# Filling TensorE in the head of a fused delta-rule and GELU kernel: early loads, products that nobody reads, a later weight transfer

## The chip, the cores and the metric

The kernel runs on one core of a Trainium2 chip. The metric is the device time of one execution, in microseconds (us). The kernel before takes 625.35 us, the median of 3 runs from 625.1 to 626.43 us. The engines are named as in the profile: PE (matrix products; PEld is its weight load), DVE (vector), ACT (scalar), POOL (GpSimd) and SP, which issues most transfers.

## The reference

```python
# q, k, v: (4, 8, 768, 48); beta: (4, 8, 768)
k_n = k / (np.linalg.norm(k, axis=-1, keepdims=True) + 1e-06)
state = np.zeros((B, H, D, D), dtype=np.float32)
for t in range(S):
    kt, vt, bt = (k_n[:, :, t], v[:, :, t], beta[:, :, t, None])
    y[:, :, t] = np.einsum('bhd,bhde->bhe', q[:, :, t], state)
    v_old = np.einsum('bhde,bhd->bhe', state, kt)
    state = state + bt[:, :, :, None] * np.einsum('bhd,bhe->bhde', kt, vt - v_old)
...
x = y.transpose(0, 2, 1, 3).reshape(B * S, H * D)      # (3072, 384)
h = x @ w_in                                           # w_in (384, 2048), float64 on input
g = 0.5 * h * (1.0 + erf(h * inv_sqrt2))
out = (g @ w_out).astype(np.float32)                   # w_out (2048, 384), float64 on input
```

The attention is a delta rule over 768 steps for 32 heads; its outputs are the tokens of a two-layer network with an exact GELU.

## The kernel before

**Chunks and units.** The 768 steps are cut into 12 chunks `c` of 64. A unit (`tiles[c, a]`) is one chunk of two batches: batch p of the pair sits on half p of the 128 partitions. Two chunks make a group `g`. `first` are the four units of chunks 0 and 1, `third` the two of chunk 2, `fourth` the two of chunk 3.

**Inside a group.** K is transposed on PE (`transposed`, L405) and multiplied with itself (`diagonals` for the 32x32 diagonal blocks of group 0, `grams` for the rest) and with Q (`queries`). Each 64x64 triangular system is inverted in two halves of 32: `eliminate_steps` (L491) scales a triangle (`scales`, on POOL), turns the diagonal blocks (`flip`, DVE L508, L513), goes through rows j = 1 to 30 with two small DVE instructions each (L528, L530), and turns the result back (`back`, L536): `back(0)` into XM, `back(1)` into the right columns of `Zf`, and in group 0 `back(2)` into the left columns of `Zf`, all three DVE transposes of 128x1024. `clear` then sets the lower left quarter of `Zf` to zero. `join` (L568) couples the two halves: at level 0 PE products that DVE scales into XM (L589), at level 1 PE products that ACT copies into `Zf` (L593). `against_state`, `solve` (psU), `use` (psY), `update` (psS) and `turn` (psX) then give the chunk's outputs, turned for the network.

**The network.** `fc1` (L909) makes psH from `w_in_sb` and the turned outputs, followed by a GELU on ACT into `G`; `fc2` (L929) makes psO from `G` and `w_out_sb`. From chunk 2 on the layers are done with fewer products, out of sums of blocks (`part_of_layer`, `second_layer`).

**The weights.** They arrive as float64 and are decoded to float32 by integer steps. A part `n` (0 to 7 of w_in, from `n_in` = 8 of w_out) goes through `fetch` (its transfers, L234), `begin` (exponent bits, DVE L252 or L255), `exponents` (ACT), `mantissas` (two DVE steps, L272 and L274) and `signed` (L281 and L282, after which the buffer is fetched into again). Where `two_kinks(n)` holds, ACT does the exponent in two steps and `signed` has no L281. The raws of w_in 0 to 3 wait in `w_out_sb`, those of w_out in `w_raw` slots.

**Order.** Up to `by_hand.close()` the order on DVE, POOL, ACT, PE and SP is that of the program text. After it a list of steps with due times (`plan`, in units of chunks) is sorted and emitted; DVE and POOL keep that order, and so does ACT where `keep` is used, while PE, SP and the rest of ACT are ordered by a scheduler, except for runs tied by `together` and `behind`. In the head SP issues, in this order: K of chunks 0, 1, beta, Q of chunks 0, 1, V of chunk 0, raws 0, 1 of w_in, K of chunk 2, Q of chunk 2 (into the buffers of chunk 0's Q), K of chunk 3 (into `Qp[2 + a]`), raws 2, 3 of w_in, raws 0 to 2 of w_out, V of chunk 1.

Of the kernel before, what the change touches and what calls it, by code (L numbers as in the profile page):

```python
# [19 lines left out]
def kernel(  # L20
# [165 lines left out]
    G = Gp[0]  # L186
    spare = Gp[1].rearrange("q a f n -> q (a f n)")
# [51 lines left out]
    def two_kinks(n):  # L239

        return 2 < n < n_in or n_in + 3 < n < n_in + 7
# [27 lines left out]
    def mantissas(n):  # L269
        dst, lo, hi, e = halves[n]  # L270
        bits = dst.bitcast(U32)
        nc.vector.tensor_scalar(bits, hi, 0xFFFFF, 0x100000, op0=ALU.bitwise_and,  # L272
                                op1=ALU.bitwise_or)
        nc.vector.scalar_tensor_tensor(dst, lo, 2.0 ** -32, bits, ALU.mult, ALU.add)  # L274
# [24 lines left out]
    def decode_in():  # L299

        marks = {3: (None, 1.05, 0.99, 1.06), 4: (1.0, 1.09, 1.1, 1.13),
                 5: (1.12, 1.18, 1.14, 1.2), 6: (1.19, 1.24, 1.21, 1.25),
                 7: (1.245, 1.3, 1.29, 1.36)}
        steps = []
        for n, (a, b, c, d) in marks.items():
            if a is not None:
                steps += [(a, (begin, n))]
            steps += [(b, (exponents, n, keep)), (c, (mantissas, n)), (d, (signed, n))]
        return steps
# [95 lines left out]
    def transposed(u, part=(0, 1)):  # L405
        for x in part:
# [10 lines left out]
            flat = (Qp[2 + u.a] if u.c == 3 and x == 0 else (u.Kp, u.Qp)[x]).rearrange("q h d -> q (h d)")  # L417
# [73 lines left out]
    def eliminate_steps(g):  # L491
# [44 lines left out]
        def back(x):  # L536
# [4 lines left out]
            elif x == 1 or g == 0:  # L541
                cols = slice(HB, C) if x == 1 else slice(0, HB)
                nc.vector.transpose(Zf[g % 2][:, :, cols].rearrange("q u i -> q i u"), nu)
# [8 lines left out]
        def clear(g):  # L552
                for cc in range(2):
                    for p in range(2):
                        part = Zf[g % 2][p * C + HB:(p + 1) * C,
                                         cc * NU // 2:(cc + 1) * NU // 2, 0:HB]
                        if g == cc == p == 0:
                            nc.scalar.mul(part, low[0:HB, 0:HB // 2], 0.0)
                        else:
                            nc.gpsimd.memset(part, 0.0)  # L560

# [3 lines left out]
        steps += [(1.9, back, x) for x in range(3)]  # L565
        return steps + [(0.0, clear, 0)] if g == 0 else steps
# [342 lines left out]
    def fc1(c, f):  # L909
# [8 lines left out]
        if c <= 1 or f < EARLY:  # L918
            keep(nc.scalar.activation, *gelu)
        else:  # L920
            nc.scalar.activation(*gelu)
# [270 lines left out]
    def signs(c0, c1):  # L1192
# [7 lines left out]

    by_hand = ExitStack()
    by_hand.enter_context(tc.manual_schedule(engines={
        mybir.EngineType.DVE, mybir.EngineType.Pool, mybir.EngineType.Activation,
        mybir.EngineType.PE, mybir.EngineType.SP}))
    load_v(0)
    for n in range(2):
        fetch(n)
    load_k(2, "Kp")
    new_group(0)
    n0 = wk.tile([128, 2 * NA, H], F32, tag="n0", name="n0", bufs=1)  # L1210
    for c in range(2):
        ns[c] = n0[:, c * NA:(c + 1) * NA]
    for u in first:
        squares(u, n0[:, u.t], nc.gpsimd if u.t == 1 else nc.vector)
        transposed(u, (0,))
        if u.t in (1, 2):
            diagonals(first[u.t - 2 + 1])
# [4 lines left out]
    scales_, flip_, *rows, back0, back1, back2, clear_ = [s_[1:] for s_ in eliminate_steps(0)]  # L1222
    factors(gms[0], beta_m[:, 0:2].rearrange("q c a h -> q (c a) h"), n0)
    scales_[0]()
    flip_[0]()
# [3 lines left out]
    signs(2, NC)  # L1229
    third = [tiles[2, a] for a in range(NA)]  # L1230
    sums_ = [(u, h) for u in third for h in range(H)]
    for u in first:
        transposed(u, (1,))
        if u.c == 1:
            for x in sums_[5 * u.a:5 * u.a + 5]:
                sum_of_squares(*x)
        queries([u])
    for a in range(NA):
        fetch_q(tiles[2, a])
    for a in range(NA):  # L1240
        fetch_in(Qp[2 + a][:, :, 0:D], k, tiles[3, a])
    for n in range(2, NS):
        fetch(n)
    for n in range(n_in, n_in + 3):
        fetch(n)
    load_v(1)
    for u in third:
        transposed(u, (0,))
    for x in sums_[10:13]:
        sum_of_squares(*x)  # L1250
    grams(third)
    for u in third:
        transposed(u, (1,))
    for x in sums_[13:]:
        sum_of_squares(*x)
    fourth = [tiles[3, a] for a in range(NA)]
    for u in fourth:
        transposed(u, (0,))
    grams(fourth)
    for fn, *args in rows:  # L1260
        fn(*args)
    nc.vector.scalar_tensor_tensor(ng, gms[0][:, 0:NA], -1.0, ns[0], ALU.mult, ALU.mult)
    back0[0](*back0[1:])
    against_state(first[:NA])
    for u in first:
        masked(u)
    back1[0](*back1[1:])
    for a in range(NA):
        join(0, (a,), 0)
    back2[0](*back2[1:])  # L1270
    for a in range(NA):
        join(0, (a,), 1)
    clear_[0](*clear_[1:])
    for u in first[NA:]:
        scale_v(u)
    begin(0)
    exponents(0)
    mantissas(0)
# [30 lines left out]
    def state_at(c, *times, first=(), second=(), last=()):  # L1309

        steps = state_steps(c, first, second, last)
        if len(times) > len(steps):
# [7 lines left out]
    plan += [at(1.06, 1.065, [(1.0, load, 3)]),  # L1320
             [(t, (join, 0, range(NA, 2 * NA), level)) for level, t in enumerate((1.085, 1.16))],
# [20 lines left out]
    plan += [at(1.36, 1.361, [(1.0, fetch, n_in + 3)]), at(1.07, 1.071, [(1.0, load_v, 2)]), at(2.727, 2.728, [(1.0, sum_of_w, 1, 2)]), at(2.96, 2.961, [(1.0, last_sum_of_w)]), at(3.07, 3.071, [(1.0, sum_of_w, 4)])]  # L1342
# [129 lines left out]
```

## Time and profile before

| | |
|---|---|
| median of 3 runs | 625.35 us (625.1 to 626.43) |
| profiled execution | 626.68 us, span 624.9 us |
| PE busy | 602.5 us (96%), mean granted clock 0.989 |
| DVE busy | 440.1 us (70%) |
| ACT busy | 241.4 us (39%) |
| POOL busy | 212.6 us (34%) |
| chain that ended last | PE 81%, DVE 14%, issue 2%, DMA 1%, ACT 1% |
| from HBM, to HBM | 33.62 MB, 4.72 MB |

Busy time is a share of the whole span; the head, up to some 75 us, has other limits than the rest, so it is read by the timelines of each engine and by windows. In a timeline a row is a run of like instructions: start, time taken, engine, line, operation, tiles, shapes, count, and in brackets the idle time of the engine before it and what ended it. "issue" there means that the profile shows nothing that the engine waited for. An fp32 product counts twice (two passes) in the trace, a transpose on PE once.

### The profile page before, as it was taken

The page shows a single profiled execution, that of the slowest core. Times are in us where ns is not written, and L with a number is a line of the kernel's source. Part 1 is how long each engine was busy: PE and PEld are TensorE (multiplying, and loading weights), DVE is VectorE, ACT ScalarE, POOL GpSimd, SP SyncE. Part 2 cuts the span into 40 slices and gives each one's busy share as a digit, 9 for nine tenths or more (in the row PEclk, how much of TensorE's full clock was granted, in tenths as well). Part 3 has the DMA queues.
Part 4 walks back from the last instruction along what each step waited for, and adds up shares of the span by engine and source line. Part 5 has one row for each costly group of instructions (what it writes and reads, how often), then busy time and mean ns, then how long its engine had stood idle before and what let it go on. Part 6 is the DMA issues. An engine that isn't in the chain of part 4 may idle for free.

```text
span 624.9 us, 19704 instructions
## 1 busy us (share of the span) xinstructions
PE 602.5 (96%) x8358; PEld 537.7 (86%) x8358; DVE 440.1 (70%) x811; ACT 241.4 (39%) x546; POOL 212.6 (34%) x316
## 2 busy tenths in 40 slices
PE   5768999999999999999999999999999999999997
PEld 4657786776899998998899998899998899988997
DVE  6999899999967697774859755859745947332532
ACT  3576877625443264224451134451134222044200
POOL 4045002100379821687222885222885200000000
PEclk9996999999999999999999999999999999999999
DMA  9793775002423452353123533013421001010011
GB/s 134 164 294 118 174 179 149 17 10 40 72 38 49 77 93 37 57 115 39 16 43 55 95 70 39 13 29 52 79 50 17 12 3 27 3 24 1 0 27 26
DMA packets 159576, 39.64 MB, mean 63 GB/s; under 512 B 151168, under 2 KB 154368, under 8 KB 159488
## 3 DMA queue, kind: packets, MB, share of 16 engines
q1 hardware_dynamic: 156816, 37.34, 30.9%
q10 hardware_dynamic: 2672, 1.03, 0.9%
q8 instruction: 66, 1.08, 0.7%
q14 instruction: 22, 0.18, 0.1%
HBM read 33.62 MB, written 4.72 MB: 61 GB/s over the span
## 4 chain that ended last, share of the span: by engine, by line
PE 81%; DVE 14%; issue 2%; DMA 1%; ACT 1%; SPq 0%; DVEq 0%
PE psX L966 13%; PE psY L1032 11%; PE psY L966 9%; PE psX L1032 9%; PE psV L1032 6%; PE psZ L1032 6%; PE psZ L966 4%; PE psV L966 4%; DVE tmp L528 3%; DVE Nu L530 3%; PE psK L732 3%; PE psO L933 3%; PE psH L915 2%; PE psY L822 2%; PE psU L792 2%
## 5 line engine op out<-in xcount | busy, mean ns | idle before, releaser
L377 POOL TENSOR_TENSOR n<-n,half 128x16 f32<-128x16 f32 x10 | 31.4, 3138 | 180.1 <-DVE n L375 130.0
L530 POOL TENSOR_TENSOR Nu<-Nu,tmp 128x30 f32<-128x30 f32 (+14 forms) x120 | 65.0, 541 | 9.4
L528 POOL TENSOR_TENSOR tmp<-Nu 128x30 f32<-128x30 f32 (+14 forms) x120 | 62.4, 520 | 9.4
L1032 PE MATMUL psX<-xT,w_in_sb 128*128 128x256 f32 (+1 forms) x288 | 62.6, 346 | 0.0
L966 PE MATMUL psX<-w_out_sb,G 128*128 128x192 f32 x320 | 56.1, 329 | 0.0
L966 PEld LDWEIGHTS psX<-w_out_sb,G 128*128 128x128 f32 x320 | 52.2, 190 | 0.7
L1032 PEld LDWEIGHTS psX<-xT,w_in_sb 128*128 128x128 f32 x288 | 47.9, 190 | 5.4
L915 PE MATMUL psH<-xT,w_in_sb 128*128 128x256 f32 x192 | 44.7, 387 | 0.7 <-ACT G L1015 0.5
L933 PE MATMUL psO<-w_out_sb,G 128*128 128x384 f32 x128 | 43.9, 490 | 0.0
L851 DVE TENSOR_TENSOR V<-psY,y 64x192 f32<-64x192 f32 (+1 forms) x60 | 21.3, 355 | 31.0 <-PE psY L834 27.0
L915 PEld LDWEIGHTS psH<-xT,w_in_sb 128*128 128x128 f32 x192 | 36.2, 192 | 7.9 <-ACT G L1015 2.3
L1060 DVE TENSOR_TENSOR psY<-psY,pu 128x512 f32<-128x512 f32 x20 | 14.0, 700 | 40.5 <-PE psY L1032 39.9
L1032 PE MATMUL psY<-xT,w_in_sb 128*128 128x256 f32 (+1 forms) x192 | 41.5, 345 | 0.0
L1015 ACT COPY xT<-psX 128x768 f32<-128x768 f32 x9 | 7.2, 799 | 79.8 <-PE psX L892 79.8
L1015 ACT COPY pu<-psZ 128x512 f32<-128x512 f32 x40 | 23.5, 587 | 37.3 <-PE psZ L1032 35.0
L933 PEld LDWEIGHTS psO<-w_out_sb,G 128*128 128x128 f32 x128 | 23.6, 190 | 14.1
L1032 PEld LDWEIGHTS psY<-xT,w_in_sb 128*128 128x128 f32 x192 | 32.1, 191 | 3.5
L1015 ACT ACTIVATE G<-G 128x512 f32<-128x512 f32 x40 | 25.2, 631 | 21.0 <-DVE G L1068 20.8
L1068 DVE TENSOR_TENSOR G<-psY,pu 128x512 f32<-128x512 f32 x20 | 13.8, 691 | 22.2 <-PE psY L1032 21.5
L1015 ACT ACTIVATE G<-psY 128x512 f32<-128x512 f32 x20 | 11.9, 596 | 45.3 <-PE psY L1032 45.3
L966 PE MATMUL psY<-w_out_sb,G 128*128 128x192 f32 x160 | 28.1, 329 | 0.0
L966 PE MATMUL psZ<-T,pu 128*128 128x192 f32 x160 | 28.1, 329 | 0.0
(207 smaller groups left out, 1370.2 us busy)
## 6 DMA issues: line engine op xcount, KB each, us to landing
Kp<-in_k_dram SPq DMA_DIRECT2D x76, 96.0 KB, 3.2
w_out_sb<-in_moe_w_in_dram SPq DMA_DIRECT2D x24, 256.0 KB, 4.0
V<-in_v_dram SPq DMA_DIRECT2D x48, 96.0 KB, 3.1
w_raw<-in_moe_w_out_dram SPq DMA_DIRECT2D x12, 384.0 KB, 7.4
out_dram<-o_sb SPq DMA_DIRECT2D x40, 96.0 KB, 2.2
Qp<-in_k_dram SPq DMA_DIRECT2D x64, 32.0 KB, 2.3
G<-in_moe_w_out_dram SPq DMA_DIRECT2D x4, 384.0 KB, 5.1
Qp<-in_q_dram SPq DMA_DIRECT2D x96, 16.0 KB, 2.0
```

The costliest lines, as they stand in the source:

```text
L377: nc.gpsimd.tensor_tensor(flat, flat, half, op=ALU.pow)
L528: rows_on.tensor_tensor(tmp, nu[:, j + 1:, j:j + 1].to_broadcast([128, n, j]), nu[:, j:j + 1, 0:j].to_broadcast([128, n, j]), op=ALU.mult)
L530: rows_on.tensor_tensor(nu[:, j + 1:, 0:j], nu[:, j + 1:, 0:j], tmp, op=ALU.add)
L732: nc.tensor.matmul(u.psK[HALF[p], r, j, :], lhsT=u.Kt[rows, p, j, :], rhs=SQ[rows, u.a, p ^ r, j, 0:w], start=True, stop=True)
L851: nc.vector.tensor_tensor(dst, src, pairs(u.y[at_], s), op=ALU.add)
L915: nc.tensor.matmul(psH, lhsT=w_in_sb[:, f // 2, m, f % 2 * 128:(f % 2 + 1) * 128], rhs=xTs[c][:, m, :], start=(m == 0), stop=(m == NM - 1))
L933: nc.tensor.matmul(u.psO, lhsT=G[:, u.a, f, :], rhs=w_out_sb[:, f, :], start=(f == 0), stop=(f == NF - 1))
L966: nc.tensor.matmul(ps_, lhsT=lhs[:, f, :], rhs=rhs[:, f, :], start=first and f == 0, stop=f == FH - 1, skip_group_check=not first)
L1015: i = fn(*args, **kw)
L1032: nc.tensor.matmul(ps_[:, i], lhsT=lhs[:, f // 2, f % 2 * 128:(f % 2 + 1) * 128], rhs=rhs, start=first and i == 0, stop=True, skip_group_c ...
L1060: nc.vector.tensor_tensor(L1["Y1"], L1["Y1"], L1["pu"][:, 0], op=ALU.add)
L1068: nc.vector.tensor_tensor(half(1, 1), shaped(L1["Y1"]), shaped(L1["pu"][:, 0]), op=ALU.add)
```

## The change

It touches the head and two helpers:

- K of chunk 3 and Q of chunk 2 go into the first half of `G` (padding zeroed by four POOL memsets), and their transfers, with K of chunk 2, are issued ahead of V of chunk 0 and w_in's raws. V of chunk 1 goes ahead of raws 2 and 3.
- `unread` issues PE products whose result nobody reads. 38 of 8x8 stand in front of the first transposes of K. Others stand between the rows of the elimination, before the join and between its levels.
- The transposes and grams of chunks 2 and 3 and the unread products are tied to rows of the elimination: `behind_rows` lets the first PE instruction of each step wait for the last DVE instruction written so far.
- The sums of squares of chunk 2 on ACT stand behind these steps.
- The third transpose of group 0 (`back(2)`) is gone; ACT copies the upper left quarter of `Zf` from the upper right (`upper_left`), chunk 0's half in the head, chunk 1's at 1.05 of the plan. The zeros are written by two POOL memsets right after the scaled triangle.
- The first three raws of w_out are fetched behind the second join's PE products.
- `two_kinks` holds for part 2 as well; `begin(0)` and half of `mantissas(0)` stand before the second half of the join's copies, which DVE takes.
- Some due times move.

```diff
+    early_q, early_k = [[G[:, a, 4 * i:4 * i + 4].rearrange("q f (e n) -> q (f e) n", n=C)
+                         for a in range(NA)] for i in range(2)]
+    for a in range(NA):
+        tiles[2, a].Qp = early_q[a]
+        for x in (early_q, early_k):
+            nc.gpsimd.memset(x[a][:, :, D:], 0.0)
...
-        return 2 < n < n_in or n_in + 3 < n < n_in + 7
+        return 1 < n < n_in or n_in + 3 < n < n_in + 7
...
-        marks = {3: (None, 1.05, 0.99, 1.06), 4: (1.0, 1.09, 1.1, 1.13),
+        marks = {3: (None, 1.08, 0.99, 1.081), 4: (1.0, 1.112, 1.1, 1.13),
...
-        steps += [(1.9, back, x) for x in range(3)]
-        return steps + [(0.0, clear, 0)] if g == 0 else steps
+        return steps + [(1.9, back, x) for x in range(3 if g else 2)]
+
+    def upper_left(us, put=lambda fn, *args: fn(*args)):
+        for p in range(2):
+            top = slice(p * C, p * C + HB)
+            put(nc.scalar.copy, Zf[0][top, us, 0:HB], Zf[0][top, us, HB:C])
...
+    def unread(*cols):
+        psI = ps.tile([128, 512], F32, tag="mlp", name="psI")
+        for n in cols:
+            wide = Kp[0].rearrange("q h d -> q (h d)") if n > 128 else ident
+            m, k = min(n, 128), HB if n < HB else 128
+            nc.tensor.matmul(psI[0:m, 0:n], lhsT=ident[0:k, 0:m], rhs=wide[0:k, 0:n],
+                             start=True, stop=True)
...
+    load_k(2, "Kp")
+    for a in range(NA):
+        fetch_q(tiles[2, a])
+    for a in range(NA):
+        fetch_in(early_k[a][:, :, 0:D], k, tiles[3, a])
     load_v(0)
     for n in range(2):
         fetch(n)
-    load_k(2, "Kp")
+    load_v(1)
+    for n in range(2, NS):
+        fetch(n)
...
+    unread(*[H] * 38)
...
+    for p in range(2):
+        nc.gpsimd.memset(Zf[0][p * C + HB:(p + 1) * C, :, 0:HB], 0.0)
...
+    between = {12: [(turned, third, 0)], 13: [(turned, third, 1)], 14: [(grams, third)],
+               15: [(unread, *[32] * 12)], 16: [(unread, *[32] * 12)], 17: [(turned, fourth, 0)],
+               18: [(unread, *[32] * 10)], 19: [(unread, *[32] * 10)], 20: [(grams, fourth)],
+               21: [(unread, 64, 64)], 22: [(unread, *[64] * 4)]}
+    between.update({j: [(unread, *[64] * 3)] for j in range(23, 26)})
+    between.update({j: [(unread, 128, 64)] for j in range(26, HB - 2)})
+    between[HB - 2] = [(unread, 128)]
     for fn, *args in rows:
         fn(*args)
+        for step in between.get(args[0], ()) if args else ():
+            behind_rows(*step)
+    for x in sums_:
+        sum_of_squares(*x)
     nc.vector.scalar_tensor_tensor(ng, gms[0][:, 0:NA], -1.0, ns[0], ALU.mult, ALU.mult)
+    behind_rows(unread, *[256] * 4)
     back0[0](*back0[1:])
...
     back1[0](*back1[1:])
+    upper_left(slice(0, NA * H))
     for a in range(NA):
         join(0, (a,), 0)
-    back2[0](*back2[1:])
-    for a in range(NA):
-        join(0, (a,), 1)
-    clear_[0](*clear_[1:])
+    unread(*[256] * 2, 128)
+    begin(0)
+    join(0, (0,), 1)
+    exponents(0)
+    mantissas(0, (0,))
+    join(0, (1,), 1, nc.vector.tensor_copy)
+    after = latest(mybir.EngineType.PE)
+    for n in range(n_in, n_in + 3):
...                                    # fetch(n); the first transfer waits for `after`
+    mantissas(0, (1,))
...
-    plan += [at(1.06, 1.065, [(1.0, load, 3)]),
-             [(t, (join, 0, range(NA, 2 * NA), level)) for level, t in enumerate((1.085, 1.16))],
+    plan += [at(1.1, 1.105, [(1.0, load, 3)]),
+             at(1.05, 1.051, [(1.0, upper_left, slice(NA * H, NU), keep)]),
+             [(t, (together, (join, 0, range(NA, 2 * NA), level))) for level, t in enumerate((1.085, 1.16))],
```

## The prediction

> **What bounds the kernel now.** I read the page first, then the chain of waits up to 140 us, then the timelines of the head engine by engine. One execution is profiled: 626.68 us, 624.9 us of it span, so 1.78 us lie around the span; it is 1.33 us above the median of the three runs, 625.35 us. I work with differences and take them off the median. A difference of about 0.2% (1.25 us) is what a measurement of this kernel can tell from none.
>
> ```profile
> PE 602.5 (96%) x8358; PEld 537.7 (86%) x8358; DVE 440.1 (70%) x811; ACT 241.4 (39%) x546; POOL 212.6 (34%) x316
> PE   5768999999999999999999999999999999999997
> PEclk9996999999999999999999999999999999999999
> ...
> q8 instruction: 66, 1.08, 0.7%
> ```
>
> PE has 22.4 us of idle time, nearly all in the first 75 us; behind that its stream is closed, and a microsecond won in the head is won at the end if nothing gives it back. The last line is the queue that carries PE's code: packets, MB, share. In the head the chain is DVE nearly without a break from 14.95 us (the transpose into Nu) to 63 us: the elimination's rows, two transposes, the join, a third transpose, then the decoding of the weights. PE runs beside it, and this is where it stalls or runs slowly:
>
> ```profile
> 11.94 0.34 PE L487 MATMUL psD<-Kt 48*32 48x32 f32 x10
> 13.63 0.80 PE L487 MATMUL psD<-Kt 48*32 48x32 f32 x54 [1.36 <-issue]
> ...
> 31.68 1.97 PE L419 MATMUL psT<-ident,Kp 128*128 128x128 f32 x8
> ...
> 38.10 1.14 PE L419 MATMUL psT<-ident,Qp 128*128 128x128 f32 x8 [2.06 <-ACT SQ L420]
> ...
> 44.99 1.95 PE L578 MATMUL psJ<-Zf,XM 32*32 32x32 f32 x64 [1.49 <-DVE XM L589]
> ```
>
> Read the pair of transposes: eight take 1.97 us at 31.68 and 1.14 us at 38.10, so PE is at its slow clock until about 34 us, although the PEclk row prints full speed there. Then it has full clock for a while only:
>
> ```profile
> 34.24:44.48 10.24, 5.32 (x196) 4.49 (x188) 9.61 (x24) 8.13 (x25) 4.41 (x5) 1.00 0.98 352
> 44.48:58.13 13.65, 11.57 (x265) 10.15 (x266) 13.37 (x17) 9.43 (x22) 10.14 (x8) 0.50 0.45 100
> ```
>
> In these stretches the columns are us, busy time of PE, PEld, DVE, ACT, POOL, then the granted clock: 1.00, and then 0.50 for 13.65 us, just when join, solve and first outputs run.
>
> ```profile
> 45.76 1.93 DVE L543 STREAM_TRANSPOSE Zf<-Nu 128x1024 f32<-128x1024 f32 x1
> ...
> 50.34 1.19 DVE L272 TENSOR_SCALAR w_in_sb<-w_out_sb 128x768 uint32<-128x768 uint32 x1
> 51.56 1.47 DVE L274 SCALAR_TENSOR_TENSOR w_in_sb<-w_out_sb,w_in_sb 128x768 f32<-128x768 uint32 x1
> ...
> 59.80 0.95 DVE L281 SCALAR_TENSOR_TENSOR w_e<-w_out_sb,w_e 128x768 uint32<-128x768 uint32 x1
> ```
>
> These are the DVE rows that the change touches.
>
> **Front, up to the first row.** The 1.36 us stall sits in the middle of one group of 64 identical products, with nothing to wait for. 1.08 MB in 66 packets are 16.4 KB each, and 16,716 PE instructions over 66 packets are 253: PE gets its code in blocks of about 256. The next unexplained stall, 0.60 us at 17.37, comes 256 instructions later (54 + 74 products with a load each), and a third, 1.58 us at 48.5, again stands a multiple of 256 behind. So a block is late when 256 short instructions run in less time than its fetch. From the instruction counts, block two was entered at about 9.1 us (in the second diagonal group) and block three was there at 13.63: 4.5 us. The 38 products of 8x8 in front add 38 x 2 x 2 = 152 instructions, which run while PE waits for K (idle until 4.47 us). Block two is then entered at about 7.1 us, block three needed at the third diagonal group, 10.76, and there at 7.1 + 4.5 = 11.6. PE loses 0.85 there and not 1.36, and the fourth diagonal ends at about 13.65, not 14.43. Nu's transpose starts near 14.1 instead of 14.95. It can't gain more than 1.1, its idle time, since the scaled triangle from POOL (14.00 + 1.91) is due for the product behind it. I take 0.7; ends: 1.1 (no stall) and -0.4 (fetch as slow as the 5.6 us between about 42.9 and 48.5 in the heaviest DMA traffic).
> The Trainium skill ("Runtime: NRT & Kernel Launch", Instruction fetch mechanics) has code streamed in 16 KiB blocks of 256 instructions, which agrees, but calls the crossing mostly hidden; the 1.36 us stall doesn't agree. By that sentence the shift would be worth 0, and the total 0.7 less.
>
> What the 38 cost: no row shows 8x8. A 48x32 product takes 13.9 ns (64 in 0.89 us), a 32x32 one of the join at slow clock 30 ns (64 in 1.95 us), a psB one 127 ns (10 in 1.27 us at 19.06 us). 76 of them are 1.1, 2.3 or 9.7 us from the identity's readiness at 1.5 us. The join is nearest (same 32 rows, as small): they end near 3.8 to 5, and K's second transposes wait until 6.01 anyway, which leaves 0.45 us of cover. Four memsets of Q and K padding are some 0.15 us each on POOL, in front of a 0.95 us idle: nothing.
>
> **K and Q of chunks 2 and 3 early.** Sixteen DMA issues go ahead of V and the first raws of w_in on SP. SP issued V from 10.93 to 14.65 and the raws to 18.2; they now start about 11 us later (2.4 + 7.2 + 2.6 from the rows of these issues, less waits that fall away), with raws landing by 33 us. POOL takes V at 40, DVE the first raw at 45.7: covered by over 5 us. PE's transposes and grams of these chunks move between rows of the elimination; the first to need those grams is the next elimination, at 111 us. The 16 sums of chunk 2 on ACT go behind them (about 3.6 us from some 38), ahead of the first copy due at 44: just covered.
>
> **Between rows: the unread products.** They take PE time that was idle, up to the join at 42.3; the last four of 256 columns are some 1.9 us (psH of the same shape: 238 ns a pass in 7.14/30, two passes), from 39.9 to 41.8. They add nothing to the path. If they keep the clock up, the second join is 1.2 (as at 42.30) instead of 1.95, solve and outputs about 2.4 instead of 4.6 (warm rows at 82.45 and 86.32: 1.15 and 2 x 0.65), the two updates 0.65 instead of 1.11 each. ACT's copies between stay (2.0 + 1.9 us). Followed through, psH of chunk 0 starts at about 53.7 instead of 56.95: PE gains 3.2.
>
> **DVE from 43.95 on, the shorter side.** Removed: the third transpose, 47.54 - 45.76 = 1.78; one sign step of raw 2 (two kinks now), 60.78 - 59.80 = 0.98. Added: two copies of 32x256 out of PSUM, by the join's 0.44 each (1.75/4), 0.88. Two ACT copies of 0.62 each take the transpose's place, in ACT's idle 2.62 us before 46.09, and the other half is paid on ACT near 58. Sum 1.88. POOL beside DVE: L272 took 0.97 and 1.19 against 0.55, L274 1.47 against 0.96 while POOL wrote Zf and scaled V, 1.57 in all. Zf's memsets go to 16 us; scaling V, 2.14 us, now starts at 46.6 behind the masks and meets the first L272 (0.64) and some of the next step (0.25). That leaves 0.7; bounds 0 and 1.57. DVE gains 2.6: the first weights are ready at 53.3, the second at 57, the fourth at 62.5 (65.37 before), and the second join of chunk 1, which waited for DVE (0.48 at 66.87), goes forward by as much.
>
> **w_out's raws behind the second join.** Six issues, 2.36 MB, move from 35.2 to 46.4 us. On SP they stand before the raws of w_in 4 and 5, issued when DVE releases their buffers (52 and 56). At the 400 GB/s of 40 to 44 us they need 6 us, so the raws of part 4 land near 58, DVE wants them near 60.9. Covered by 2.9 us; w_out is first wanted near 78.
>
> **Sum.** 0.7 + 2.6 = 3.3, DVE setting it; PE could give 3.2 + 0.7. Behind 68 us PE and DVE stand to each other as before. 625.35 - 3.3 = 622.0.
>
> **Rivals.** (a) The clock falls all the same between 46 and 54 us, when PE waits for ACT's copies. For it: in 51.3 to 54.7 PE was busy without a gap and the clock still stayed at 0.50, so small products count little. Against: it fell only after a stretch with 1.20 us of work in 3.41. PE then runs its 8.46 us from solve to psH as before from 46.5, psH starts at 55 and catches up as the clock returns near 58: 1.2 + 0.7 gained, 623.4.
> The Trainium skill ("TensorE: Matmul & The Clock Gate", Part 1) has the clock fall after one idle window of 3.4 us that runs freely; the trace agrees with the length (10.24 and 13.65 are three and four of them), but the last window here was not idle.
> (b) The head's gain is given back: raws of w_in come late behind w_out's, or the moved code boundaries stall PE elsewhere. One more stall is 1 to 1.6; with the DMA slack gone too, about 2.7: 624.7.
> (c) Block three comes at the same moment wherever the boundary lies (its fetch hangs on the DMA traffic, not on PE's progress), so the stall only moves and DVE's 2.6 alone is left: 622.75. Against: three stalls, all a whole number of blocks apart.
> The hidden fetches of the Trainium skill's page on the runtime, above, would give this time too.
> (d) Slower: the 38 products are still running when K is there. They decide from 5.0 us on; at 90 ns a pass (8.3 us) they eat the whole gain, at the 127 ns of psB they end at 11.2, 6.2 us late, and 625.35 - 2.6 + 6.2 = 629.0. Against: psB loads 128 columns, these load 8.
>
> **Chances.** Forecast 0.60, (a) 0.15, (b) 0.10, (c) 0.05, (d) 0.10. The forecast's own range is 620.3 (1.1 + 1.88 + 1.57 = 4.55, and some of PE's surplus) to 623.8 (-0.4 + 1.88). With (a), (c) and most of (b) the range is 620.3 to 625.0. Faster 0.78: forecast, (a), (c) and little less; same 0.11, mostly (b); slower 0.11.
>
> **What would show it.** Right: no or a shorter issue stall in psD before 13 us, Nu's first transpose near 14.2; granted clock 1.00 from 44 to 58; psH of chunk 0 near 53; DVE's fourth signed step near 62; raws of part 4 landed before DVE asks. Wrong: a first transpose of K behind 5 us, PE waiting for issue at psU or psX, a clock of 0.50 after 46 us, DVE waiting for DMA near 60.

## The result, and the profile after

The changed kernel is slower. Its median is 630.54 us (630.14 to 631.74, 4 runs) beside 625.64 us for the kernel before (625.1 to 626.43, 4 runs on the same chip): ratio 1.0081, 95% interval 1.0066 to 1.0096, some 5 us. The profiled execution took 631.74 us with a span of 630.0, 5.1 more than the span before.

The page of the changed kernel, the lines that answer to those shown before:

```profile
PE 612.1 (97%) x8584; PEld 546.3 (87%) x8584; DVE 438.7 (70%) x811; ACT 243.2 (39%) x548; POOL 212.1 (34%) x319
PE   6997999999999999999999999999999999999997
PEclk9996999999999999999999999999999999999999
...
q8 instruction: 67, 1.10, 0.7%
```

PE is busier in the second and third slices (7 and 6 tenths before, 9 and 9 now), as meant, but less busy in the fourth (8 before, 7 now), and it is 9.6 us busier in all; filling PE is not the same as ending earlier. Where the time goes is seen when the same events are laid side by side (us from the span's start):

| event | before | after | difference |
|---|---|---|---|
| Nu's first transpose | 14.95 | 16.41 | +1.46 |
| first decode step of part 0 | 47.54 | 47.18 | -0.36 |
| first psU | 48.52 | 48.40 | -0.12 |
| psU of the second unit | 49.66 | 50.78 | +1.12 |
| psH of chunk 0 | 56.95 | 60.21 | +3.26 |
| part 0 signed | 54.91 | 55.31 | +0.40 |
| part 2 signed | 61.74 | 62.77 | +1.03 |
| part 3 signed | 65.37 | 70.21 | +4.84 |
| Nu's transpose in group 1 | 111.33 | 116.05 | +4.72 |
| first join of group 1 | 138.58 | 143.26 | +4.68 |

The loss is complete by 70 us and is carried nearly unchanged from there. Three places stand out, and a fourth behind them on DVE. First the timeline of PE, changed kernel (start, time, engine, line, operation, tiles, shapes, count, idle before it and what ended that):

```profile
1.53 2.05 PE L1206 MATMUL psI<-ident 32*8 32x8 f32 x76 [1.53 <-POOL ident masks.py:199]
...
11.81 0.88 PE L495 MATMUL psD<-Kt 48*32 48x32 f32 x64 [1.21 <-ACT Kt L428]
...
12.98 0.88 PE L495 MATMUL psD<-Kt 48*32 48x32 f32 x62
15.66 0.31 PE L495 MATMUL psD<-Kt 48*32 48x32 f32 x2 [1.80 <-issue]
...
44.34 1.20 PE L580 MATMUL psJ<-XM,G 32*32 32x32 f32 x64
...
48.40 0.68 PE L794 MATMUL psU<-V,Zf 64*64 64x48 f32 x32 [0.41 <-POOL P L482]
50.78 1.11 PE L794 MATMUL psU<-V,Zf 64*64 64x48 f32 x32 [1.70 <-DVE Zf L595]
...
58.07 0.34 PE L836 MATMUL psS<-V,Kp 64*64 64x48 f32 x2 [2.09 <-issue]
...
60.21 6.20 PE L917 MATMUL psH<-xT,w_in_sb 128*128 128x256 f32 x18
```

The profile puts the 1.21 us before the third diagonal group (11.81) down to ACT; `e1_front36` below shows that it is a stall of the same kind as the next. The 1.80 us stall stands before the last product (two passes) of the fourth diagonal group, and the whole front waits for that product. In the solve, PE waits 1.70 us for DVE's copies into `Zf`. In the first update it stops for 2.09 us, again with one product left. Then the timeline of DVE, changed kernel:

```profile
16.41 1.95 DVE L516 STREAM_TRANSPOSE Nu<-diag 128x1024 f32<-128x1024 f32 x1 [2.23 <-ACT diag L497]
...
47.18 1.35 DVE L261 TENSOR_SCALAR w_e<-w_out_sb 128x768 uint32<-128x768 uint32 x1
48.45 1.18 DVE L279 TENSOR_SCALAR w_in_sb<-w_out_sb 128x768 uint32<-128x768 uint32 x1
49.66 0.86 DVE L595 COPY Zf<-psJ 32x256 f32<-32x256 f32 x2
...
69.25 0.96 DVE L290 SCALAR_TENSOR_TENSOR w_in_sb<-w_in_sb,w_e 128x768 f32<-128x768 f32 x1 [4.08 <-ACT w_e L1014]
```

The copies that the solve needs (L595) stand behind two decode steps, which take 2.53 us here beside POOL. And DVE stands still for 4.08 us at part 3, waiting for its exponents from ACT. Who made ACT late is in the timeline of ACT, changed kernel:

```profile
63.18 0.39 ACT L1014 ACTIVATE G<-psH 128x256 f32<-128x256 f32 x1 [1.40 <-PE psH L917]
65.16 0.38 ACT L1014 ACTIVATE G<-psH 128x256 f32<-128x256 f32 x1 [1.60 <-PE psH L917]
65.44 1.23 ACT L1014 COPY Zf<-Zf 32x512 f32<-32x512 f32 x2
66.69 0.38 ACT L1014 ACTIVATE G<-psH 128x256 f32<-128x256 f32 x1
67.10 2.13 ACT L1014 ACTIVATE w_e<-w_e,lim 128x768 f32<-128x768 int32 x2
```

The exponents (the last row) now come behind three GELUs and the two copies of `upper_left`; the GELUs wait for psH, which is late and slow. The clock, in windows of the changed kernel (us, busy time of PE, PEld, DVE, ACT, POOL, then granted clock, DMA share, GB/s):

```profile
47.34:50.75 3.41, 1.33 (x72) 1.12 (x64) 3.32 (x5) 2.61 (x6) 3.41 (x4) 1.00 0.52 161
50.75:54.16 3.41, 3.38 (x97) 3.27 (x98) 3.38 (x5) 1.89 (x7) 2.44 (x1) 0.50 0.84 272
```

The clock is up from 23.44 to 50.75 us, and in the kernel before from 34.24 to 44.48. It rose 8 us ahead of the first product between rows (31.58), so the fill can only have held it. In the first window shown PE has 1.33 us of work, since it waits for the copies; the clock falls at its end and stays at 0.50 until 64.40, with psH in that stretch.

### The profile page after: what moved, and what is told of

Same layout as the page of the kernel before. It is cut to its first block, busy times and chain, and to the rows that moved or that the text cites. A ratio compares the mean times of both kernels' runs of the same rounds, so it can differ in the third digit from the quotient of the medians.

```text
span 630.0 us, 20185 instructions
## 1 busy us (share of the span) xinstructions
PE 612.1 (97%) x8584; PEld 546.3 (87%) x8584; DVE 438.7 (70%) x811; ACT 243.2 (39%) x548; POOL 212.1 (34%) x319
## 3 DMA queue, kind: packets, MB, share of 16 engines
q10 hardware_dynamic: 2672, 1.03, 0.8%
HBM read 33.62 MB, written 4.72 MB: 61 GB/s over the span
## 4 chain that ended last, share of the span: by engine, by line
PE 82%; DVE 13%; issue 3%; ACT 1%; POOL 1%; DVEq 0%; POOLq 0%
PE psX L965 12%; PE psY L1031 11%; PE psY L965 9%; PE psX L1031 8%; PE psV L1031 6%; PE psZ L1031 6%; PE psV L965 4%; PE psZ L965 4%; PE psH L917 3%; DVE Nu L538 3%; DVE tmp L536 3%; PE psK L734 3%; PE psO L932 3%; PE psY L824 2%; PE psU L794 2%
## 5 line engine op out<-in xcount | busy, mean ns | idle before, releaser
L917 PE MATMUL psH<-xT,w_in_sb 128*128 128x256 f32 x192 | 46.5, 397 | 1.0 <-ACT G L1014 1.0
L965 PE MATMUL psX<-T,G 128*128 128x192 f32 x160 | 28.0, 327 | 0.8 <-issue 0.8
```

The lines of the kernel that those rows point to most:

```text
L917: nc.tensor.matmul(psH, lhsT=w_in_sb[:, f // 2, m, f % 2 * 128:(f % 2 + 1) * 128], rhs=xTs[c][:, m, :], start=(m == 0), stop=(m == NM - 1))
L965: nc.tensor.matmul(ps_, lhsT=lhs[:, f, :], rhs=rhs[:, f, :], start=first and f == 0, stop=f == FH - 1, skip_group_check=not first)
```

## Where a code block ends

The stalls put down to "issue" can be placed. In the built program a product counts four PE instructions (two passes, each with its load), a transpose two, a lone wait one. Counted that way, every such stall up to 20 us lies at PE instruction 193 + 256 x k, in both kernels; later stalls are placed one by one, since some that are put down to "issue" are waits of another kind (the 1.18 us ahead of the transposes at 28.09 in the changed kernel stands at a lone wait for a row of the elimination). In the kernel before, 449 is 20 instructions into the fourth diagonal group (its 1.36 us) and 705 is in the grams. In the changed kernel 449 is at the start of the third diagonal group and 705 lies 124 instructions into the 128 of the fourth: one product is left on the far side. The stall of 2.09 us is at 2497. The 38 unread products moved the boundary from the harmless grams into the last product of the diagonals.

## Experiments

Each run is set against the kernel before on the same chip; that one's medians were 626.1 (first four), 625.98 (next four), 626.37 (next four) and 625.84 us (last four).

**One cause at a time.** First theory: four separate losses, each undone by one edit. Rival: the clock's fall makes most of the loss, whatever the edit.

`e1_front36`, two unread products fewer, so that 705 falls behind the diagonals:

```diff
-    unread(*[H] * 38)
+    unread(*[H] * 36)
```

> The changed kernel with 36 instead of 38 unread products in front of K. Theory A (code blocks of 256 PE instructions, boundaries at 193, 449, 705, ... counted over products with four instructions, transposes with two and lone waits with one): with 38 the boundary 705 lies 124 instructions into the 128 of the fourth diagonal group, whose last two products then waited 1.80 us; with 36 it lies 4 into the next group. The fourth diagonal ends near 13.9 instead of 15.9, Nu's transpose starts near 14.4 instead of 16.41, and the whole kernel gains about 2.0 us: 628.5. Theory B (the stall comes from the DMA traffic at that moment, not from the place of the boundary): the stall stays within the fourth diagonal and the time within 0.5 us of 630.5.

627.03 us, ratio 1.0011 (0.9999 to 1.0023). Timeline of PE, `e1_front36`:

```profile
10.59 0.25 PE L495 MATMUL psD<-Kt 48*32 48x32 f32 x4
11.67 0.71 PE L495 MATMUL psD<-Kt 48*32 48x32 f32 x60 [0.83 <-issue]
...
12.55 0.76 PE L495 MATMUL psD<-Kt 48*32 48x32 f32 x64
13.24 0.43 PE L448 MATMUL psG<-Kt 48*64 48x64 f32 x2
15.79 3.47 PE L448 MATMUL psG<-Kt 48*64 48x64 f32 x119 [2.12 <-issue]
```

The stall is still there, longer even, but one product behind the diagonals, where nobody waits: Nu's transpose starts at 14.10 and not 16.41. The boundary 449 has moved too, four passes into the third group, and the stall with it; those four run at 10.59, so the group's data was there and the wait was for code. Two products of 8x8 are worth 0.7% of the time, about 4.4 us. Not all of that is the front's: the first psU starts 2.2 us earlier (46.21), but the edit moves every later boundary by eight instructions as well, 2497 falls into psX and costs 1.41 us there in place of 2.09, and psH starts 3.3 us earlier. DVE's wait for ACT is as before (4.07 us).

`e2_exp_early`, due times of parts 3 and 4 as in the kernel before:

```diff
-        marks = {3: (None, 1.08, 0.99, 1.081), 4: (1.0, 1.112, 1.1, 1.13),
+        marks = {3: (None, 1.05, 0.99, 1.06), 4: (1.0, 1.09, 1.1, 1.13),
```

> The changed kernel with the due times of part 3's and part 4's exponents and signed steps as before (1.05, 1.06, 1.09, 1.13 instead of 1.08, 1.081, 1.112, 1.13). Theory A (DVE's 4.08 us of idle time at 65.2 is ACT's queue: the two exponent steps stand behind three GELUs and two Zf copies): the idle time falls under 1 us and the kernel gains 3 to 4 us: 627. Theory B (PE, at half clock until 64.4, is as late by itself: its first join product of chunk 1 starts at 66.34 against 61.60 before): the idle time goes, but PE's second join of chunk 1 moves by 0.5 us at most, and so does the kernel: 630.

628.41 us, 1.0044 (1.0028 to 1.006). DVE's wait at part 3 is 0.3 us, and the gain is 2.3 us by the ratios. In the profiled execution the clock rose for good only at 36.4 us; PE was still busy with the fill when the join was due, and DVE waited 2.50 us for psJ. What the gain would be without that wait is not shown.

`e3_raws_early`, w_out's raws at the place before:

```diff
-    after = latest(mybir.EngineType.PE)
     for n in range(n_in, n_in + 3):
...                                    # fetch(n), right behind w_in's raws, no wait
```

> The changed kernel with w_out's first raws issued right behind w_in's raws, without the wait for the second join. Theory A (the 2.09 us issue stall at 58.07 is the code block behind boundary 2497, whose transfer stood behind the raws: entered at 50.6, fetched only from 55.72): without the raws from 48 to 55 the block is there in time, psH starts about 2 us earlier (58.1) and the kernel gains 2 to 3 us: 628. Block 1985 or 2241 is late instead, near the join, where PE has 0.4 to 1.7 us to spare. Theory B (the half clock and ACT's queue set the time): psH earlier by 2, the kernel within 0.7 us of 630.5.

628.66 us, 1.0032 (1.0013 to 1.0052). The stall in the update is gone: the waits of PE between 40 and 62 us, `e3_raws_early`, are only

```profile
PE psU L794 <- DVE Zf L595: 0.7, 1, 0.7
PE psU L794 <- POOL V L410: 0.4, 1, 0.4
```

So the six transfers issued at 48.0 held up PE's code: in the changed kernel the code transfer for block 2497 starts only at 55.72, though the block before was entered near 50.6; here it starts at 53.15, 2 us behind the entry. The edit is worth some 3 us alone.

`e4_copies_act`, both pairs of the second join's copies on ACT:

```diff
     join(0, (0,), 1)
+    join(0, (1,), 1)
     exponents(0)
     mantissas(0, (0,))
-    join(0, (1,), 1, nc.vector.tensor_copy)
```

> The changed kernel with both halves of the second join copied by ACT, ahead of the exponents of part 0, and none by DVE. Theory A (solve's second unit waited 1.70 us for DVE's copies, which stand behind two decode steps that POOL slows to 1.35 and 1.18 us): it starts near 49.2 instead of 50.56, DVE is 0.9 us shorter, and the kernel gains about 1.5 us: 629. Theory B (the code block behind 2497 comes when the raws are through, whenever it was asked for): the 1.4 us turn up in a longer issue stall near 57, and the kernel stays within 0.5 us of 630.5.

628.86 us, 1.0041 (1.0026 to 1.0055). The second unit's psU follows the first by 0.77 us and not 2.38, and the clock is low for 3.4 us only. The fill was late here too (psJ at 46.33, 1.71 us of waiting).

The four gains, 4.4, 2.3, 3.1 and 2.5 us by the ratios, add up to 12.3 where 5 were lost: they overlap. In the profiled executions psH starts 3.3, 0.8, 1.8 and 1.9 us earlier, 7.8 together, where the change had lost 3.26.

**All together, and the clock.** `e5_all_four` has the four edits:

```diff
-    unread(*[H] * 38)
+    unread(*[H] * 36)
...                                    # marks as in e2, raws as in e3, copies as in e4
```

> The changed kernel with all four edits of the first experiments at once: 36 products in front of K, part 3's and 4's exponents as early as before, w_out's raws where they were, both halves of the second join copied by ACT. Theory A (four causes in different places, each worth 2 to 3 us alone, partly the same microseconds): about 2 us below the kernel before, 624. Theory B (the clock's fall around 51 us, when PE waits for ACT's copies, is the common cause, and the single edits only moved it): the granted clock falls again near 50, and the kernel ends near the kernel before, 625.5 to 626.5.

624.53 us, 0.998 (0.9969 to 0.9991): a little faster than before. Both of the next stand on these four edits: `e6_all_no_fill` also takes out the products between rows, before the join and between its levels, `e8_all_warm` adds some instead:

```diff
-               15: [(unread, *[32] * 12)], 16: [(unread, *[32] * 12)], 17: [(turned, fourth, 0)],
...
-    behind_rows(unread, *[256] * 4)
...                                    # e8: unread(*[256] * 2) behind the solve and behind the use
```

> The kernel with the four edits, and without any unread product between the rows, before the join and between its levels (the 36 in front stay, and so do the transposes and grams tied to rows). Theory A (the fill is what keeps the clock up through join and solve): the clock falls near 44 as in the kernel before, solve and outputs run at half clock, and the kernel is 2 to 3 us slower than with the fill. Theory B (PE's queue gains nothing from it and is sometimes still busy with it when XM is there: 0.85 us in the changed kernel, 2 to 4 us where the clock came up late): as fast as with the fill, or up to 2 us faster.

> The kernel with the four edits and two unread products of 256 columns each behind solve's products and behind use's, in PE's waits for ACT. Theory A (the clock falls near 51 because PE idles there): it stays at 1.00 until the end, the network's first products run at 238 ns a pass from the start, and the kernel gains 1 to 2 us over the four edits alone. Theory B (small products and waits are not what the clock falls by, or it falls by the phase of a free-running window): it falls all the same in this stretch, and the four products cost up to 1 us.

`e6_all_no_fill`: 625.23 us, 0.9993 (0.9984 to 1.0003); the clock is at 0.50 for 23.9 us from 36.1, and the medians are 0.7 us apart, with intervals that overlap. `e8_all_warm`: 625.27 us, 0.9996 (0.9982 to 1.0011); the clock is at 1.00 from 29.9 us on, and it is no faster: psH starts at 56.32, 2.05 us later than in `e5_all_four` (54.27). Of this 1.14 us is there already at the first psU, ahead of the first added product; whether the rest is what the added products cost is not shown. The rival falls: the kernel before and the change have the same 13.65 us at 0.50 and lie 5 us apart, and with 23.9 us of it `e6_all_no_fill` ties with the kernel before.

`e7_before_two_transposes` is the kernel before with the third transpose replaced by the two ACT copies, nothing else:

```diff
-            elif x == 1 or g == 0:
+            elif x == 1:
...                                    # upper_left on ACT in its place
```

> The kernel before with one part of the change: the third transpose of group 0 replaced by the two ACT copies (upper left from upper right, all 32 units at once). Theory A (DVE sets the time from 44 to 66 us): begin of part 0 at 45.8 instead of 47.5, and the kernel 1.5 to 1.8 us faster: 624. Theory B (PE's own chain from the second join to psH at half clock sets it): psH starts up to 1.1 us earlier, since POOL's zeros no longer wait for the transpose, and the kernel gains 0 to 1.

625.34 us, 0.9998 (0.9985 to 1.001). Part 0 is signed 1.47 us earlier and psH starts 1.1 us earlier, but no gain can be measured at the end. The first psU does not move (48.56). The profile puts its wait of 2.02 us down to POOL, but POOL's zeros for that chunk are done at 47.09; what ends 0.10 us ahead of psU is ACT's share of the zeros (`clear`, 47.83 to 48.46), which stands behind ACT's four copies of the join.

**Which of the four are needed.** All in this group have the 36 products.

`e9_raws_last`: early exponents, ACT copies, and the raws of w_out only behind part 2.

```diff
+    for n in range(n_in, n_in + 3):
+        fetch(n)                       # behind signed(2), no wait
```

> 36 products in front, early exponents and ACT copies as in the kernel with the four edits, but w_out's raws issued only at the end of the head, behind the signed step of part 2. Theory A (PE's code blocks come late when the raws travel, whether early (1.34 us in solve, boundary 2241) or behind the second join (2.09 us at boundary 2497)): no issue stall above 0.7 us between 40 and 58 us, psH 1 to 1.5 us earlier than with the four edits, and 1 us off the total: 623.5 against 626 of the kernel before. Theory B (a block's time is its own latency of about 4 us, with or without the raws): the stall in solve stays above 1 us and the total within 0.4 us of the four edits, 624.5.

630.54 us, 1.0078 (1.0047 to 1.0108): as slow as the change, for other reasons. (The profiled execution, 633.63 us, is the slowest of its four.) No code stall is left in solve and outputs, but DVE waits for raws. The waits of DVE from 42 to 110 us, `e9_raws_last` (total, times, longest):

```profile
DVE XM L591 <- PE psJ L580: 4.2, 1, 4.2
DVE w_in_sb L290 <- ACT w_e L1014: 2.7, 2, 1.8
DVE w_e L258 <- DMA w_raw<-in_moe_w_out_dram: 1.8, 1, 1.8
DVE w_e L258 <- DMA w_out_sb<-in_moe_w_in_dram: 1.3, 1, 1.3
```

The transfers can be too late as well as too early; the 4.2 us is the fill again, with the clock up from 31.3 us.

`e10_before_front36`: the kernel before with 36 products of 8x8 in front.

```diff
+    psI = ps.tile([128, 512], F32, tag="mlp", name="psI")
+    for n in range(36):
+        nc.tensor.matmul(psI[0:H, 0:H], lhsT=ident[0:HB, 0:H], rhs=ident[0:HB, 0:H],
+                         start=True, stop=True)
```

> The kernel before with nothing changed but 36 unread products of 8x8 in front of the first transposes of K. Theory A (boundary 705 now lies behind the fourth diagonal group): Nu's first transpose near 14.1 instead of 14.95, so DVE is 0.9 us earlier; the total gains 0.5 to 0.9 us against the kernel before. Theory B (the later boundaries move too, and 1985 now falls 10 instructions into psY instead of into psS): the gain is lost again by a stall of 1 to 2 us there, and the total is the same or up to 1 us slower.

628.69 us, 1.0042 (1.0028 to 1.0056). Nu's transpose starts at 14.04, 0.91 earlier, as the theory has it; yet the kernel is 2.6 us slower. The waits of PE from 40 to 62 us, `e10_before_front36`:

```profile
PE psU L792 <- POOL Zf L560: 1.5, 1, 1.5
PE psJ L578 <- issue: 1.1, 1, 1.1
PE psY L822 <- issue: 0.6, 1, 0.6
```

The 144 instructions moved two later boundaries as well: 1729 falls into the join and 1985 into psY. Code in front moves every boundary behind it. The first row names POOL, whose zeros for this chunk are done at 48.91; psU starts at 49.46, and ACT's share of the zeros (L558) ends at 49.36. The same is seen in the timeline of ACT, kernel before:

```profile
46.98 0.74 ACT L593 COPY Zf<-psJ 32x256 f32<-32x256 f32 x2
47.79 0.63 ACT L558 ACTIVATE Zf<-G 32x512 f32<-32x512 f32 x1
```

L558 ends at 48.42 and psU starts at 48.52, again 0.10 us behind it. So the 1.58 us at psU in the kernel before, where "issue" stood, was no code stall: boundary 1729 is 26 instructions into psU, and the stall is ahead of psU, where PE waited for ACT.

`e11_three_exp_late` has 36, the early raws and ACT copies; `e12_three_raws_join` has 36, early exponents and ACT copies, the raws as in the change:

```diff
-    unread(*[H] * 38)
+    unread(*[H] * 36)
+    join(0, (1,), 1)
-    join(0, (1,), 1, nc.vector.tensor_copy)
...                                    # e11: raws early; e12: marks as in e2
```

> The four edits less one: the exponents of parts 3 and 4 at the late due times of the changed kernel. Theory A (ACT's queue): DVE waits 3 to 4 us for ACT before part 3's signed step, against 0.9, and the kernel is 1.5 to 3 us slower than with the four edits. Theory B (with PE in time, the GELUs in front of the exponents are done early, and their place in ACT's queue costs nothing): within 0.5 us of the four edits.

> The four edits less one: w_out's raws behind the second join, as in the changed kernel. Theory A (raws): an issue stall of 1.5 to 2 us at boundary 2497, in the turn of the second unit, and 1 to 2 us more than the four edits. Theory B (that block is late only where the clock is low): no stall there above 0.7 us, same time as the four edits.

`e11_three_exp_late`: 626.1 us, 0.9997 (0.9986 to 1.0007), DVE waits 1.9 us for the exponents. `e12_three_raws_join`: 624.18 us, 0.997 (0.9957 to 0.9984), clock 1.00 from 22.6 us to the end. With front and copies mended, the later place of the raws costs nothing that can be seen, though PE still loses 1.3 us at 2497, now in psX.

**Two edits.** What was open: whether front and copies alone account for the loss, and whether the place of the boundary, not the number of products, sets the front.

`e13_front44` has 44 products in place of 38, which puts 705 at instruction 100 of 128 of the fourth diagonal group and 449 at 115 of 128 of the second:

```diff
-    unread(*[H] * 38)
+    unread(*[H] * 44)
```

> The changed kernel with 44 unread products in front. Theory A (place of the boundary): boundary 705 lies 100 instructions into the fourth diagonal group, its last products wait again, now from an earlier entry into the block (449 in the second group), so Nu's first transpose comes at 15 to 16 us, later than the 14.1 of 36 products, and the kernel is 1 to 2 us slower than with 36 (627). Theory B (the number of products, or the moment they end): 44 lies on the other side of 38 from 36, so it is at least as late as 16.4.

630.75 us, 1.0071 (1.0044 to 1.0098). Timeline of PE, `e13_front44`:

```profile
9.21 0.83 PE L495 MATMUL psD<-Kt 48*32 48x32 f32 x57
11.58 0.33 PE L495 MATMUL psD<-Kt 48*32 48x32 f32 x7 [1.54 <-issue]
...
14.05 0.77 PE L495 MATMUL psD<-Kt 48*32 48x32 f32 x50
15.63 0.36 PE L495 MATMUL psD<-Kt 48*32 48x32 f32 x14 [0.80 <-issue]
```

Nu's transpose starts at 16.48, later than the 15 to 16 that I wanted, so by this number alone "more products, later" fits as well. The rows decide: both stalls stand where the count put them, 57 and 50 passes into their groups, and fewer products (36) did not shorten the stall but moved it.

`e14_front_copies` is the change with 36 products and the ACT copies; `e15_front_exp` is the change with 36 products and the early exponents:

```diff
-    unread(*[H] * 38)
+    unread(*[H] * 36)
...                                    # e14: copies as in e4; e15: marks as in e2
```

> The changed kernel with 36 products in front and ACT copies, exponents still late. Theory A (copies behind DVE's decode carry the rest): solve's second unit follows the first by 0.8 us instead of 2.4, and the kernel comes within 0.5 us of the three edits together (0.997 of the kernel before). Theory B (the exponents' place carries it): DVE still waits 2 to 4 us for ACT, and the kernel is 1.5 us slower than with the three, 0.9995 of the kernel before.

> The changed kernel with 36 products in front and early exponents, DVE copies as in the change. Theory A (the copies carry the rest): solve's second unit waits 1.7 us for DVE, psH starts about 1.5 us later than with the three edits, and the kernel is at the kernel before, 0.9995. Theory B (the exponents' place carries it): within 0.5 us of the three edits, 0.997.

`e14_front_copies`: 624.5 us, 0.9986 (0.9959 to 1.0012). Its profiled execution took 622.64 us (span 620.9); windows:

```profile
20.70:54.00 33.30, 30.00 (x775) 25.09 (x776) 31.40 (x66) 25.68 (x78) 12.34 (x9) 1.00 0.76 211
54.00:70.00 16.00, 15.11 (x182) 11.76 (x182) 15.26 (x23) 13.28 (x22) 0.00 (x0) 1.00 0.85 235
```

The clock does not fall from 20.7 us on, psH starts at 53.73, part 3 is signed at 62.06 though its exponents have the late due time, with 0.3 us of waiting. `e15_front_exp`: 626.72 us, 1.001 (0.9988 to 1.0032), no better than `e1_front36` without the early exponents. So front and copies alone undo the loss (0.9986 beside 1.0081), and the late exponents are not a loss by themselves. What they cost when psH is late is not settled: undoing them alone gave 2.3 us (`e2_exp_early`), but on top of the front it gave nothing that can be measured, although DVE's wait of 4.07 us went.

`e16_three_pool_copy` is `e12_three_raws_join` with chunk 1's copies of `upper_left` on POOL:

```diff
-             at(1.05, 1.051, [(1.0, upper_left, slice(NA * H, NU), keep)]),
+             at(1.05, 1.051, [(1.0, upper_left, slice(NA * H, NU),
+                               lambda fn, *args: nc.gpsimd.tensor_copy(*args))]),
```

> The three edits, and chunk 1's upper left quarter of Zf copied by POOL instead of ACT (POOL is idle from 53 us on). Theory A (PE waits 1.4 us for a GELU near 62, since ACT has 1.2 us of copies and two steps of exponents in front of it): the wait falls under 0.5 us and the kernel gains 0.5 to 1 us on the three edits, 0.9955 of the kernel before. Theory B (DVE sets the time there): same as the three edits, or slower by what POOL's copies cost DVE's steps beside them.

623.82 us, 0.9961 (0.994 to 0.9982), the best version: about 2 us under the kernel before. It is not told apart from `e12_three_raws_join` by the intervals. Its profiled execution, 625.6 us, is the slowest of its ten; DVE, `e16_three_pool_copy`:

```profile
47.13 1.75 DVE L591 TENSOR_TENSOR XM<-psJ,gm 32x256 f32<-32x256 f32 x4 [3.94 <-PE psJ L580]
```

The clock rose at 33.2 us there, so the fill tied to the rows ran late and the join waited for it. In `e5_all_four`, `e12_three_raws_join` and `e14_front_copies` it rose at 20.7 to 22.6 us, and the join started at 42.

## Why the prediction was wrong

It said 622.0 us, 3.3 less than before, with a range of 620.3 to 625.0; it came out 5 us more than before.

**Front: the step that failed first.** The term was -0.7 and measured +1.46. The mechanism was right, and so was the first half of the working: the next block was there at 11.81 where I had 11.6, and PE went on from the very group I had named (it lost 1.21 us there where I had 0.85). What I left out is the boundary after it. I let the fourth diagonal run through to 13.65 and did not ask where the next 256 instructions end; they end one product short, and the block came at 15.66. Rival (c), "the stall only moves", was nearer in kind than the forecast, but even it had no stall that lands worse than the old one. Rival (b), "the moved code boundaries stall PE elsewhere", named what happened, with a chance of 0.10 and one stall in its price; two came. One of the three stalls that the forecast rested on was misread besides: the 1.58 us at 48.5 is not at a boundary, but 26 instructions ahead of one, and was a wait for ACT. The Trainium skill ("Runtime: NRT & Kernel Launch", Instruction fetch mechanics) has code refilled in blocks of 256 instructions, one fetched while the other runs; the count agrees exactly. Its "mostly hidden" does not: 1.80 and 2.09 us in one run.

**The 38 products** were no danger: 76 passes took 2.05 us, 27 ns each, a little less than the 2.3 us that the join's row gave, and were done by 3.6 us, before K's first transposes at 4.50. Rival (d) had the right sign by the wrong mechanism.

**Early K and Q** landed in time, as worked out.

**The fill between rows** I costed at nothing, in idle PE time. In the profiled execution of the change the join started 0.80 us after XM was there (43.54), behind the products of 256 columns. Those took 1.89 us, as priced, but began at 42.52, 1.1 us after the DVE instruction that they are tied to: the products of 64 and 128 columns ahead of them, which I had not followed, still ran (5.47 us from 37.21). In the profiled executions where the clock rose only at 31 to 36 us, DVE waited 1.7 to 4.2 us for that join. The row I had priced the fill by ran at full clock.

**The clock.** Rival (a) came true in its place (0.15 I gave it): it fell after a window in which PE waited for copies, though the longest wait (1.70 us) was for DVE's copies and not for ACT's. But the size was off. I had PE catch up; instead psH began 3.26 us later than before and ran at half clock. In `e6_all_no_fill`, which has a longer fall but also none of the fill's own delay, the two come out about even (0.7 us between the medians).

**DVE's 2.6 us.** Up to the first decode step it was nearly right: the third transpose's 1.78 less the front's 1.46 gives -0.32, measured -0.36. Then the term for POOL (0.7 in all) failed: L261 and L279 took 2.53 against 1.10, 1.43 over, where the steps of the kernel before were 1.57 over, so the term came to 0.14. The two copies took 0.86, as priced. Part 0 was signed 0.40 later, where I had 1.6 earlier: 1.46 of these 2.0 us are the front's and 0.56 POOL's. And I costed the copies on DVE as DVE time only, not as the wait they put on the solve behind two decode steps: 1.70 us on PE. Putting them on ACT gave 2.5 us alone and 1.6 us on top of the front (0.25% by the ratios, intervals that overlap).

**"Some due times move"** is a line of the change which I passed over. It put part 3's exponents behind GELUs, and showed as the largest wait of DVE, 4.08 us. `e14_front_copies` shows that this is a consequence: it needs a late psH.

**w_out's raws.** DVE never waited for w_in's, as predicted. But I asked only which data would be late, not whose code: PE's block stood behind those transfers. That is rival (b)'s "code boundaries stall PE elsewhere", whose price for one stall (up to 1.6) was too small by 0.5 here.

**What was right about the whole.** With two edits, `e14_front_copies` in its profiled execution does what the forecast describes: psH at 53.73 (I had 53.7), fourth signed step at 62.06 (62.5), full clock, 622.64 us (622.0). Its median, 624.5, stays 1.9 above, and that execution is one of the three fastest of its ten, so the near hit of the total is partly luck.

**Shown**: the front's boundary (2.2 us at the first psU, 4.4 us for the edit with what follows from it and with the later boundaries that it moves), the copies on DVE, the raws' hold on the code block. **Open**: how the rest splits between copies, exponents and raws, whose effects overlap; how much of the 4.4 us comes from the later boundaries; and what makes single executions of `e14_front_copies` range from 622.58 to 629.67. That this is the moment at which the clock rises fits the profiled executions (one for each kernel: where it rose for good by 23 us DVE did not wait for the join, where it did so only at 31 us or later it waited 1.7 to 4.2 us), and was not tested.

## What to carry to other kernels

Where short instructions run faster than code arrives, a boundary of code is a place in the schedule: count instructions to each one, the next as well as the one being moved, and put them where nobody waits for the engine; every instruction added in front moves all that follow. A copy moved to another engine is priced by who waits for it behind that engine's queue, not by its own time. A wait that shows as the longest (here 4.08 us of exponents) may be only where an earlier delay surfaces: mend the earliest one and look again.

## What the runs showed of the chip

- PE's code boundaries lie at instruction 193 + 256 x k. From the start of a code transfer to PE going on took 2.4 to 3.1 us (8.85 to 11.81, 13.05 to 15.66, 55.72 to 58.07; before: 10.58 to 13.63). A transfer started 1.2 us after the block before was entered (11.81 to 13.05) and, behind w_out's raws, 5 us after it (50.6 to 55.72).
- What a stall costs depends on where it lands: 1.80 us inside the diagonals put Nu's transpose at 16.41, 2.12 us just behind them left it at 14.10.
- In the changed kernel the clock fell after a window of 3.41 us with 1.33 us of PE work, and did not come back after one with 3.38 us of small products. The Trainium skill ("TensorE: Matmul & The Clock Gate", Part 1) counts windows of about 3.4 us, idle or busy. The trace agrees on their length; neither of these two windows fits by PE's busy time.
- DVE's integer step of 128x768, 0.55 us alone, took 1.35 and 1.18 us beside POOL's steps of 128x512 and 128x384, and ended 0.41 and 0.42 us after the POOL step that ran when it started (48.11 and 49.21). Beside POOL's step of 128x16 (from 50.28) it took 0.55 us.
